# A fourth tile for outgoing attention rows, and a later place for the first expert's weights, in a kernel that runs banded attention and a top-1 mixture of experts

## The chip, the cores and the metric

The kernel runs on one core of one Trainium2 chip. The metric is the time of one execution in device microseconds. Three executions of the kernel before were timed, and one was taken by the hardware profiler.

## The reference

Attention first: 8 batches, 8 heads, 576 positions, head size 64. Heads 0 to 3 see the last 32 positions, heads 4 to 7 every fourth one of the last 128. The result, 4608 rows of 512, goes into a mixture of 8 experts: each row picks one.

```python
scores = scale * np.matmul(q, k.transpose(0, 1, 3, 2))
scores = np.where(masks[None], scores, -1e9)          # plain window, or dilated by 4
attn = np.exp(scores - scores.max(-1)); attn /= attn.sum(-1) + 1e-9
x = np.matmul(attn, v)  ->  [4608, 512]
logits = x @ w_gate + modality_bias[modality_id]      # [4608, 8]
e_idx = argmax(logits);  gate_w = softmax(logits)[e_idx]
for e in range(8):                                    # w1 [512, 1024], w2 [1024, 512] per expert
    out[mask] = gate_w[mask] * (np.maximum(x[mask] @ w1[e], 0) @ w2[e])
```

## The kernel before, in words

**Attention** is cut into 72 units, nine per batch (m = 0 to 8), and two units make a pair. A loop over `t` = 0 to 35 (and a few rounds more to drain) works three pairs at once: scores of pair t, exponentials of pair t - 1, products with V and normalization of pair t - 2. `state['t']` is 2t, so a time "62" in the code means pair 31. The order of PE, DVE, ACT and SP is written out by hand; each engine takes its instructions in that order.

In one round the order is: scores (PE) and the addition of the mask (DVE, L438); the product with V; loads of queries and of V for the next batch (SP); a first call of the background tasks (`advance`); the maximum (DVE, L444) with its subtraction on GpSimd; normalization (DVE, L399), which writes the rows into a tile `x_sb`; transposes of K and Q for the next batch (PE, L351, from the load tile `st`); copies (L514, L521, L149); a second and a third call of the background tasks around the turn of the probabilities; then `keep`, in which SP sends finished `x_sb` tiles to the buffers `x_dram` (L412 to L422); loads of K (SP); and a fourth call of the background tasks. So the rows of a pair are sent near the end of the round in which they are normalized. `x_sb` has three buffers and five are taken per batch; a new one can be written once the transfer out of the third one back has landed.

**Background tasks** do the gating of finished batches: they scatter each token into a list in DRAM (`table`). After batch 2, four early slots of 256 rows of one expert each are formed from what is known by then; the rest is routed after the last batch. A slot's rows come by indirect DMA into `xr`, go out to `x_slot` (L807), and come back as `xg` (L813) in another order; `prepare_x` transposes them on DVE (L962) and splits them into a high and a low part (L968, L971).

**The first slot** is served by `first_slot`, one of those background tasks: twelve steps of its weights are issued on SP at set times, by `load_more(0, 1)`, each of which runs the generator `fetch_weights` to its next `yield`. A step is either one quarter (256 KB) of a half of w1 (`half`, L828) or one pair of row blocks of w2 (`pair`, 512 KB, L833). The twelve steps are, in order: w2 pair 0; four quarters of w1's first half; w2 pairs 1 and 2; four quarters of w1's second half; w2 pair 3. While it waits for the next time, and once the time is past 63, the task also steps `prepare_x` for slot 0.

**Experts.** From pair 35 on, `slots` runs between attention's last instructions and then alone: per slot eight blocks f, each with twelve products for h and six for the output, in three terms of high and low parts. Weights are split on ACT (L980) and DVE (L981) just before use: block f uses a quarter of a half of w1 and half of a pair of w2. Weights of later slots are issued by `ahead` in the slot before, and are skipped where the expert stays the same.

**Queues.** All loads, weights and outgoing rows are issued on SP; only the gathers and scatters go through GpSimd.

Of the kernel before, what the change touches and what calls it, by code (L numbers as in the profile page):

```python
# [10 lines left out]
F32 = mybir.dt.float32  # L11
F32R = mybir.dt.float32r
BF16 = mybir.dt.bfloat16
I32 = mybir.dt.int32
# [8 lines left out]
B, H, S, D = 8, 8, 576, 64  # L23
NT = B * S
DM = H * D
NE = 8
# [9 lines left out]
GB = 96  # L36
NGB = S // GB
# [21 lines left out]
def kernel(  # L59
# [160 lines left out]


    nc.gpsimd.memset(gat.tile([P, 2, DM], F32, name="xr", bufs=1), 0.0)
    zero = cpool.tile([1, DM // 2], F32, name="zero")
    nc.gpsimd.memset(zero, 0.0)

    def constants():

        for _ in range(5):
            yield
        nc.scalar.copy(out=wgs[:, :, 0:NE], in_=wg)  # L230
        yield
        yield
        mid_t = spare[1][0:B, 0:S]
        for i in range(2):
            for a in range(2):
                nc.vector.tensor_copy(out=mid_t.rearrange("b (a c i j) -> b a i c j", a=2, c=2, i=2)[:, a, i],
                                      in_=mid[i][:, :, 0].rearrange("b (j c a) -> b a c j", c=2, a=2)[:, a])
        sent = spare[1][:, S:S + (NE + 1) * NT * 3 // P].bitcast(I32)
        nc.gpsimd.memset(sent, SENT)
        yield  # L240
        yield
        got = []

        def turn(po):
            for c in range(NGB):
                nc.tensor.transpose(out=po[0:GB, 1, ROUTE + B * c:ROUTE + B * (c + 1)], in_=mid_t[:, GB * c:GB * (c + 1)], identity=ident[:B, :B])
            got.append(po[0:GB, 1, ROUTE:ROUTE + NBLK])
        yield from on_po(turn)
        pm = got[0]
        mid_f = cpool.tile([GB, NBLK], F32, name="mid_f")  # L250
        nc.vector.tensor_copy(out=mid_f.rearrange("p (b c) -> p c b", c=NGB), in_=pm.rearrange("p (c b) -> p c b", b=B))
        yield
        yield
        mid_n = cpool.tile([GB, NBLK], F32, name="mid_n")
        nc.vector.tensor_scalar(out=mid_n, in0=mid_f, scalar1=-1.0, scalar2=1.0, op0=ALU.mult, op1=ALU.add)
        mtmp = spare[1][0:GB, S + (NE + 1) * NT * 3 // P:S + (NE + 1) * NT * 3 // P + NE * NBLK].rearrange("p (e c) -> p e c", c=NBLK)
        nc.gpsimd.tensor_tensor(out=mterm, in0=mid_n.rearrange("p (o c) -> p o c", o=1).broadcast_to([GB, NE, NBLK]),
                                in1=bias_sb[:, 0, :].rearrange("p (e o) -> p e o", o=1).broadcast_to([GB, NE, NBLK]), op=ALU.mult)
        nc.gpsimd.tensor_tensor(out=mtmp, in0=mid_f.rearrange("p (o c) -> p o c", o=1).broadcast_to([GB, NE, NBLK]),
                                in1=bias_sb[:, 1, :].rearrange("p (e o) -> p e o", o=1).broadcast_to([GB, NE, NBLK]), op=ALU.mult)  # L260
        nc.gpsimd.tensor_tensor(out=mterm, in0=mterm, in1=mtmp, op=ALU.add)
        yield
        yield
        nc.sync.dma_start(out=table.rearrange("(p a) t -> p (a t)", p=P), in_=sent)

        nc.gpsimd.iota(pay[:, :, 2], pattern=[[GB, NBLK]], base=0, channel_multiplier=1)
        place = cpool.tile([GB, 2, NBLK], I32, name="place")
        nc.gpsimd.iota(place[:, 0], pattern=[[0, B], [GB, NGB]], base=0, channel_multiplier=1)
        nc.gpsimd.iota(place[:, 1], pattern=[[S, B], [0, NGB]], base=0, channel_multiplier=0)
        ewt_i = cpool.tile([GB, NE, NGB], I32, name="ewt_i")  # L270
        nc.gpsimd.iota(ewt_i, pattern=[[-1, NE], [0, NGB]], base=NE, channel_multiplier=0)
        eoff_i = cpool.tile([GB, NE, NGB], I32, name="eoff_i")
        nc.gpsimd.iota(eoff_i, pattern=[[NT, NE], [0, NGB]], base=0, channel_multiplier=0)
        yield
        yield
        nc.vector.tensor_copy(out=ewt, in_=ewt_i)
        nc.vector.tensor_copy(out=eoff, in_=eoff_i)
        nc.gpsimd.memset(ones_bf, 1.0)
        nc.gpsimd.affine_select(out=upper, in_=ones_bf, pattern=[[1, GB]], compare_op=ALU.is_gt,
                                fill=0.0, base=0, channel_multiplier=-1)  # L280
        for t in x_dram:
            nc.sync.dma_start(out=t[NT:NT + 1, :], in_=zero)
        placef = cpool.tile([GB, 2, NBLK], F32, name="placef")
        nc.vector.tensor_copy(out=placef, in_=place)
        past = cpool.tile([GB, NBLK], F32, name="past")
        nc.vector.tensor_scalar(out=placef[:, 1], in0=placef[:, 0], scalar1=float(NCLS), scalar2=None, op0=ALU.mult)
        for r in range(1, NCLS):
            nc.vector.tensor_scalar(out=past, in0=placef[:, 0], scalar1=float(CL * r), scalar2=float(NCLS * CL - (2, -1, 2)[r - 1]), op0=ALU.is_ge, op1=ALU.mult)
            nc.vector.tensor_tensor(out=placef[:, 1], in0=placef[:, 1], in1=past, op=ALU.subtract)
        yield  # L290
        yield
        nc.vector.tensor_copy(out=place[:, 0], in_=placef[:, 1])
        nc.vector.tensor_tensor(out=pay[:, :, 0], in0=place[:, 0], in1=place[:, 1], op=ALU.add)
        yield
        yield
        nc.vector.tensor_copy(out=sid_all[:, :, 0], in_=sidx_i)
        nc.vector.tensor_scalar(out=sid_early[:, :, 0], in0=sid_all[:, 0:EARLY[0][1], 0], scalar1=-1.0, scalar2=float(EARLY[0][1] - 1), op0=ALU.mult, op1=ALU.add)
# [68 lines left out]
    class Unit:  # L366
# [23 lines left out]
        def finish(self, pov, den):  # L390
            if self.m in (1, 3, 6, 8):
                self.xs = state['xs']
            else:
                self.xs = state['xs'] = awk.tile([P, 2, 4 * D], F32, name="x_sb", bufs=3)
            if self.m < 5:
                xo = self.xs[:, self.m % 2].rearrange("p (a g d) -> p g a d", g=2, a=2)
            else:
                xo = self.xs.rearrange("p a (e g d) -> p e g a d", e=2, g=2)[:, self.hp]
            nc.vector.tensor_tensor(out=xo, in0=pov[:, :, 1:VB - 1].rearrange("p g (a d) -> p g a d", a=2),  # L399
                                    in1=den.rearrange("p g (a o) -> p g a o", o=1).broadcast_to([P, 2, 2, D]), op=ALU.mult)  # L400
# [416 lines left out]
    def fetch_weights(si, first):  # L817

        e = nc.sync.value_load(si[0:1, 0:1], min_val=0, max_val=NE - 1)
        kw = {}  # L820
        if not first:
            kw = dict(cond=nc.sync.value_load(si[0:1, 2:3], min_val=0, max_val=1), cond_hint=False)
        w1v = w1[ds(e, 1)].rearrange("o (r m p) f -> (o r) p m f", r=KC, p=BLK)

        def half(i):
            cols = slice(HALFF * P * i, HALFF * P * (i + 1))
            for r in range(KC):
                nc.sync.dma_start(out=w1q[i][BLK * r:BLK * (r + 1)], in_=w1v[r, :, :, cols], **kw)  # L828
                if first and r < KC - 1:
                    yield  # L830

        def pair(c):
            nc.sync.dma_start(out=w2q[c], in_=w2[ds(e, 1), 2 * P * c:2 * P * (c + 1), :].rearrange("o (a p) m -> p (o a) m", p=P), **kw)  # L833
            yield from ()

        for piece, i in ((pair, 0), (half, 0), (pair, 1), (pair, 2), (half, 1), (pair, 3)):
            yield from piece(i)
            yield

# [30 lines left out]
    def load_more(n, pieces):  # L870

        if n not in loads_of and n in si_of:
            loads_of[n] = [fetch_weights(si_of[n], n == 0), 0]
        if n in loads_of:
            for _ in range(min(pieces, 6 - loads_of[n][1])):
                next(loads_of[n][0], None)
                loads_of[n][1] += 1

    def first_rows(n, at):
# [7 lines left out]
        fetching.extend([(n, rows)] * n)  # L887
        todo['rows'] = max(todo['rows'], n + 1)

    def first_slot():  # L890

        prep = prepare_x(0, ids_of[0])
        for n, at in enumerate((46, 50, 52, 54, 56, 60, 62, 64, 65, 66, 67, 68)):
            while state['t'] < at:
                if state['t'] > 63:
                    next(prep, None)
                yield
            load_more(0, 1)
            loads_of[0][1] = max(n - 5, 1)
            yield  # L900
        yield from prep

# [257 lines left out]
    for t in range(NPAIR + 4):  # L1160
# [81 lines left out]
        if 0 <= t - 2 < NPAIR:  # L1242
            for unit in pairs[t - 2].units:
                unit.keep(nc.sync)
        load_next(t, here, k)
        advance([*round_of, B - 1] if moe and here else range(-1, B))
        if t == NPAIR + 2:
            octx.close()
# [45 lines left out]
```

## Time and profile before

| | |
|---|---|
| three executions | 693.64, 702.48, 708.86 us (median 702.48) |
| profiled execution, its own time | 694.29 us |
| its span, first to last instruction | 692.3 us |
| granted TensorE clock, mean | 0.969 |
| PE / PEld / DVE / ACT / POOL busy | 94 / 82 / 70 / 56 / 37 % |
| DMA | 131,677 packets, 99.12 MB, mean 143 GB/s |

PE is TensorE's matmuls and PEld its weight loads, DVE is VectorE, ACT ScalarE, POOL GpSimd, SP SyncE. A row of a timeline has the start, the time, engine, line, operation, output and input, and in brackets how long the engine stood idle before it and what ended that. A row of waits has the sum, how often, and the longest. Lines are those of the kernel before.

### The profile page before, as it was taken

How to read it: one execution, taken by the hardware profiler on the slowest of the kernel's cores; microseconds unless marked ns; L12 is line 12 of the kernel's file. 1: busy time of each engine (PE TensorE's matmuls, PEld its weight loads, DVE VectorE, ACT ScalarE, POOL GpSimd, SP SyncE). 2: the span in 40 equal slices, each digit the busy share in tenths (PEclk: the TensorE clock that was granted, in tenths of full speed). 3: DMA queues.
4: the chain of work that ended last, by engine and by line, in shares of the span. 5: the costliest groups of instructions: out<-in, count | busy, mean ns of one | idle time of the engine just before them, and what ended most of it. 6: DMA issues, size and time to landing. Idle time of an engine off the chain costs nothing. (4 is left out here: it accounts for less than half of the span.)

```text
span 692.3 us, 17695 instructions
## 1 busy us (share of the span) xinstructions
PE 648.2 (94%) x6462; PEld 566.8 (82%) x6462; DVE 483.4 (70%) x1074; ACT 384.5 (56%) x754; POOL 259.5 (37%) x315
## 2 busy tenths in 40 slices
PE   7899999998968899869999999999999999999994
PEld 4688887887757788759999999899999999889983
DVE  4768878887746866936766686667766776677652
ACT  1646765665534545434666565565666566556552
POOL 8423555645645635743312331333223341311110
PEclk9989999999978999998999999999999999999998
DMA  9966879879897434775322336743232326921560
GB/s 201 219 182 174 218 131 214 205 137 208 191 221 210 136 52 101 152 164 171 113 72 77 107 121 170 213 108 123 73 102 86 107 95 151 254 95 63 134 163 12
DMA packets 131677, 99.12 MB, mean 143 GB/s; under 512 B 67760, under 2 KB 111794, under 8 KB 131588
## 3 DMA queue, kind: packets, MB, share of 16 engines
q1 hardware_dynamic: 120500, 78.11, 46.5%
q0 software_dynamic: 8048, 19.20, 9.6%
q8 instruction: 52, 0.85, 0.5%
q10 hardware_dynamic: 3040, 0.65, 0.5%
q14 instruction: 37, 0.30, 0.2%
HBM read 127.52 MB, written 29.39 MB: 227 GB/s over the span
## 5 line engine op out<-in xcount | busy, mean ns | idle before, releaser
L981 DVE TENSOR_TENSOR w2l<-w2q,w2h 128x512 fp32r<-128x512 f32 x152 | 104.8, 689 | 41.7 <-ACT w2h L980 34.0
L1012 PE MATMUL py<-w2h,hh 128*128 128x512 f32 x296 | 119.3, 403 | 0.0
L1012 PE MATMUL py<-w2h,hl 128*128 128x512 f32 x296 | 117.5, 397 | 0.0
L313 POOL DMA_INDIRECT xr<-x_dram,idt x74 | 81.4, 1100 | 94.3 <-DMA x_slot<-xr 44.3
L313 POOL DMA_INDIRECT out_dram<-ys,idt x37 | 42.4, 1145 | 198.2 <-ACT ys L1015 122.1
L1012 PE MATMUL py<-w2l,hh 128*128 128x512 f32 x296 | 116.2, 392 | 0.0
L981 DVE TENSOR_TENSOR w1l<-w1q,w1h 128x512 fp32r<-128x512 f32 x152 | 103.8, 684 | 12.5 <-ACT w1h L980 12.5
L980 ACT CAST w1h<-w1q 128x512 fp32r<-128x512 f32 x152 | 94.6, 622 | 13.4 <-DMA w1q<-in_moe_w_dram 13.4
L1032 PE MATMUL pt<-xh,w1h 128*128 128x256 f32 (+1 forms) x320 | 91.4, 286 | 6.7 <-ACT w1h L980 6.7
L980 ACT CAST w2h<-w2q 128x512 fp32r<-128x512 f32 x152 | 93.1, 613 | 0.0
L1032 PE MATMUL pt<-xh,w1l 128*128 128x256 f32 (+1 forms) x320 | 91.4, 286 | 1.0 <-DVE w1l L981 1.0
L1032 PE MATMUL pt<-xl,w1h 128*128 128x256 f32 (+1 forms) x320 | 90.7, 283 | 0.0
L1032 PE MATMUL ph<-xh,w1l 128*128 128x256 f32 (+1 forms) x288 | 81.1, 282 | 1.7 <-DVE w1l L981 1.6
L1032 PE MATMUL ph<-xl,w1h 128*128 128x256 f32 (+1 forms) x288 | 80.9, 281 | 0.0
L1032 PE MATMUL ph<-xh,w1h 128*128 128x256 f32 (+1 forms) x288 | 80.8, 281 | 0.0
L1038 ACT ACTIVATE hh<-pt 128x256 fp32r<-128x256 f32 (+1 forms) x80 | 30.3, 378 | 88.5 <-PE pt L1032 88.5
L313 POOL TENSOR_TENSOR sm<-sm,nmx 128x768 f32<-128x768 f32 x36 | 52.9, 1470 | 57.2 <-DVE den L469 38.5
L1032 PEld LDWEIGHTS pt<-xh,w1h 128*128 128x128 f32 x320 | 61.3, 192 | 11.0 <-ACT w1h L980 7.3
L1038 ACT ACTIVATE hh<-ph 128x256 fp32r<-128x256 f32 (+1 forms) x72 | 27.1, 377 | 76.8 <-PE ph L1032 76.8
L1012 PEld LDWEIGHTS py<-w2l,hh 128*128 128x128 f32 x296 | 56.1, 190 | 13.9
L1032 PEld LDWEIGHTS pt<-xl,w1h 128*128 128x128 f32 x320 | 61.3, 192 | 3.1
L1032 PEld LDWEIGHTS pt<-xh,w1l 128*128 128x128 f32 x320 | 61.5, 192 | 2.0 <-DVE w1l L981 2.0
(197 smaller groups left out, 1304.7 us busy)
## 6 DMA issues: line engine op xcount, KB each, us to landing
w2q<-in_moe_w_dram SPq DMA_DIRECT2D x76, 512.0 KB
w1q<-in_moe_w_dram SPq DMA_DIRECT2D x152, 256.0 KB
x_slot<-xr SPq DMA_DIRECT2D x18, 512.0 KB
xg<-x_slot SPq DMA_DIRECT2D x72, 128.0 KB
x_dram<-x_sb SPq DMA_DIRECT2D x32, 256.0 KB
st<-in_k_dram SPq DMA_DIRECT2D x32, 144.0 KB
vw<-in_v_dram SPq DMA_DIRECT2D x16, 288.0 KB
st<-in_k_dram SPq DMA_DIRECT2D x8, 576.0 KB
```

Source lines behind the costliest of these rows:

```text
L313: ins = tc.keep_in_program_order(getattr(nc.gpsimd, name)(*args, **kw))
L980: nc.scalar.copy(out=hi, in_=raw)
L981: nc.vector.tensor_tensor(out=lo, in0=raw, in1=hi.bitcast(F32), op=ALU.subtract)
L1012: nc.tensor.matmul(out=py[u], lhsT=ht[:, us], rhs=wt, start=(f + n == 0), stop=(f + n == FC + 1))
L1032: nc.tensor.matmul(out=ph, lhsT=wt[:, c, :], rhs=xt[:, c, 0:cols], start=(c + i == 0), stop=(c + i == KC + 1))
L1038: nc.scalar.activation(out=hh, in_=ph, func=AF.Relu)
```

## The change

`x_sb` gets four buffers instead of three. The room for it comes from small tiles of the setup (`mid_f`, `mid_n`, `place`, `ewt_i`, `eoff_i`, `placef`, `past`), which now lie in w1's first buffer behind the modality ids, and from the row of zeros, which is now read from the tile of the warm-up products.

The first slot's steps come in a new order, at new times, and from another place. Order: four quarters of w1's first half, w2 pair 0, four quarters of w1's second half, w2 pairs 1, 2 and 3. They are issued by `first_weights`, which runs near the end of a round, after `keep` and the load of K and before the fourth call of the background tasks. The task `first_slot` only fills the list of times and, once the time is past 63, steps `prepare_x` at each call.

| step | before, round t | after, round t |
|---|---|---|
| w1 first half, 4 quarters | 25, 26, 27, 28 | 24, 25, 26, 27 (ends) |
| w2 pair 0 | 24 | 31 (end) |
| w2 pairs 1, 2 | 30, 31 | 34 (end) |
| w1 second half, 4 quarters | 32, 33, 33, 34 | 32, 32, 33, 33 (ends) |
| w2 pair 3 | 34 | 34 (end) |

```diff
-    zero = cpool.tile([1, DM // 2], F32, name="zero")
-    nc.gpsimd.memset(zero, 0.0)
+    zero = warm[0:1].bitcast(F32)
+    room = [S * 2]
+
+    def setup(shape, dtype):
+
+        n = shape[1] * (shape[2] if len(shape) > 2 else 1)
+        room[0] += n
+        t = spare[0][0:shape[0], room[0] - n:room[0]]
+        t = t if dtype is F32 else t.bitcast(dtype)
+        return t.rearrange("p (a b) -> p a b", a=shape[1]) if len(shape) > 2 else t
...
-        mid_f = cpool.tile([GB, NBLK], F32, name="mid_f")
+        mid_f = setup([GB, NBLK], F32)
...
-                self.xs = state['xs'] = awk.tile([P, 2, 4 * D], F32, name="x_sb", bufs=3)
+                self.xs = state['xs'] = awk.tile([P, 2, 4 * D], F32, name="x_sb", bufs=4)
...
-        for piece, i in ((pair, 0), (half, 0), (pair, 1), (pair, 2), (half, 1), (pair, 3)):
+        order = ((half, 0), (pair, 0), (half, 1), (pair, 1), (pair, 2), (pair, 3)) if first else ((pair, 0), (half, 0), (pair, 1), (pair, 2), (half, 1), (pair, 3))
+        for piece, i in order:
             yield from piece(i)
             yield
...
+    ending = []
+
+    def first_weights():
+
+        while ending and ending[0][1] <= state['t']:
+            load_more(0, 1)
+            loads_of[0][1] = max(ending.pop(0)[0] - 5, 1)
+
     def first_slot():
 
         prep = prepare_x(0, ids_of[0])
-        for n, at in enumerate((46, 50, 52, 54, 56, 60, 62, 64, 65, 66, 67, 68)):
-            while state['t'] < at:
-                if state['t'] > 63:
-                    next(prep, None)
-                yield
-            load_more(0, 1)
-            loads_of[0][1] = max(n - 5, 1)
+        ending.extend(enumerate((46, 50, 52, 54, 62, 64, 64, 66, 66, 68, 68, 68)))
+        while len(ending) > 3:
+            if state['t'] > 63:
+                next(prep, None)
             yield
         yield from prep
...
         load_next(t, here, k)
+        first_weights()
         advance([*round_of, B - 1] if moe and here else range(-1, B))
```

More of the change, by code (lines that the diff above doesn't have):

```diff
@@ L253, in constants @@
         yield
-        mid_n = cpool.tile([GB, NBLK], F32, name="mid_n")
+        mid_n = setup([GB, NBLK], F32)
         nc.vector.tensor_scalar(out=mid_n, in0=mid_f, scalar1=-1.0, scalar2=1.0, op0=ALU.mult, op1=ALU.add)
@@ L266, in constants @@
         nc.gpsimd.iota(pay[:, :, 2], pattern=[[GB, NBLK]], base=0, channel_multiplier=1)
-        place = cpool.tile([GB, 2, NBLK], I32, name="place")
+        place = setup([GB, 2, NBLK], I32)
         nc.gpsimd.iota(place[:, 0], pattern=[[0, B], [GB, NGB]], base=0, channel_multiplier=1)
         nc.gpsimd.iota(place[:, 1], pattern=[[S, B], [0, NGB]], base=0, channel_multiplier=0)
-        ewt_i = cpool.tile([GB, NE, NGB], I32, name="ewt_i")
+        ewt_i = setup([GB, NE, NGB], I32)
         nc.gpsimd.iota(ewt_i, pattern=[[-1, NE], [0, NGB]], base=NE, channel_multiplier=0)
-        eoff_i = cpool.tile([GB, NE, NGB], I32, name="eoff_i")
+        eoff_i = setup([GB, NE, NGB], I32)
         nc.gpsimd.iota(eoff_i, pattern=[[NT, NE], [0, NGB]], base=0, channel_multiplier=0)
@@ L282, in constants @@
             nc.sync.dma_start(out=t[NT:NT + 1, :], in_=zero)
-        placef = cpool.tile([GB, 2, NBLK], F32, name="placef")
+        placef = setup([GB, 2, NBLK], F32)
         nc.vector.tensor_copy(out=placef, in_=place)
-        past = cpool.tile([GB, NBLK], F32, name="past")
+        past = setup([GB, NBLK], F32)
         nc.vector.tensor_scalar(out=placef[:, 1], in0=placef[:, 0], scalar1=float(NCLS), scalar2=None, op0=ALU.mult)
```

## The prediction

> **What bounds the kernel now.** I read the page first (which engine is full), then the stages, then the waits, then the timeline around the longest wait.
>
> ```profile
> span 692.3 us, 17695 instructions
> PE 648.2 (94%) x6462; PEld 566.8 (82%) x6462; DVE 483.4 (70%) x1074; ACT 384.5 (56%) x754; POOL 259.5 (37%) x315
> ```
> ```profile
> 65.00:151.00 86.00, 83.42 (x1587) 71.75 (x1577) 73.20 (x212) 55.54 (x102) 45.46 (x59) 1.00 0.82 179
> 151.00:219.00 68.00, 55.87 (x960) 47.29 (x958) 42.66 (x115) 33.02 (x59) 35.54 (x44) 0.90 0.90 209
> 340.00:692.00 352.00, 341.83 (x2189) 308.73 (x2188) 240.22 (x423) 205.86 (x426) 89.44 (x81) 0.99 0.41 117
> ```
>
> The columns are the stretch, its length, PE, PEld, DVE, ACT and POOL busy, then PE's granted clock, the DMA share and GB/s. PE sets the time in most of the run: from 340 us on it is busy 341.83 of 352. No line of the change works there. The one long stretch with room is the second half of attention, 151 to 219: PE is idle 68.00 - 55.87 = **12.1 us**, the clock falls to 0.90, and the DMA engines are busy 0.90 of the time. Between 65 and 151, with the same work and no weights, PE was idle 2.6 of 86. So 12.1 us, plus what the clock costs, is all that this change can win.
>
> The pairs of units show the same. One score addition (L438) opens each pair t = 0 to 35:
>
> ```profile
> 65.40 0.96 DVE L438 TENSOR_TENSOR sm<-pss,masks 128x768 f32<-128x768 f32 x1
> ...
> 150.92 0.96 DVE L438 TENSOR_TENSOR sm<-pss,masks 128x768 f32<-128x768 f32 x1
> ...
> 194.05 0.96 DVE L438 TENSOR_TENSOR sm<-pss,masks 128x768 f32<-128x768 f32 x1
> ...
> 209.20 0.96 DVE L438 TENSOR_TENSOR sm<-pss,masks 128x768 f32<-128x768 f32 x1 [2.71 <-PE pss L436]
> ...
> 218.78 0.95 DVE L438 TENSOR_TENSOR sm<-pss,masks 128x768 f32<-128x768 f32 x1
> ...
> 229.15 0.95 DVE L438 TENSOR_TENSOR sm<-pss,masks 128x768 f32<-128x768 f32 x1
> ```
>
> These are pairs 9, 24, 31, 32, 33 and 35. From 9 to 24 a pair takes 85.5 / 15 = 5.7 us; from 24 to 31, 43.1 / 7 = 6.2; pair 31 takes 15.2 and pair 32 takes 9.6. The waits of DVE and PE in attention say on what:
>
> ```profile
> DVE x_sb L399 <- DMA x_dram<-x_sb: 13.8, 7, 6.1
> ```
> ```profile
> PE pss L351 <- DMA st<-in_k_dram: 3.9, 1, 3.9
> PE pss L351 <- DMA st<-in_q_dram: 1.6, 2, 1.4
> ```
> ```profile
> 155.25 0.42 DVE L399 TENSOR_TENSOR x_sb<-po,den 128x256 f32<-128x256 f32 x1 [1.51 <-DMA x_dram<-x_sb]
> ...
> 173.61 0.76 DVE L399 TENSOR_TENSOR x_sb<-po,den 128x256 f32<-128x256 f32 x2 [2.80 <-DMA x_dram<-x_sb]
> ...
> 204.28 0.42 DVE L399 TENSOR_TENSOR x_sb<-po,den 128x256 f32<-128x256 f32 x1 [6.10 <-DMA x_dram<-x_sb]
> ...
> 210.26 0.95 DVE L444 TENSOR_REDUCE nmx<-sm 128x8 f32<-128x768 f32 x1
> ...
> 212.92 0.76 DVE L149 COPY vw<-vw 32x520 f32<-32x520 f32 x2
> 216.77 0.71 DVE L962 STREAM_TRANSPOSE xt<-xg 128x512 f32<-128x512 f32 x1 [3.09 <-DMA xg<-x_slot]
> ```
> ```profile
> 201.19 0.87 PE L351 MATMUL pss<-ident,st 96*128 96x96 f32 x4 [3.90 <-DMA st<-in_k_dram]
> 203.47 0.90 PE L351 MATMUL pss<-ident,st 96*128 96x96 f32 x4 [1.42 <-DMA st<-in_q_dram]
> ```
>
> DVE stops 13.8 us in seven places because the third tile back has not been written out. But at the longest, 6.10 until 204.28, PE stands too, for keys until 201.19 and queries until 203.47. **Two waits lie side by side there, and both are for the same queue.** What fills it is in SP's order of issue (start, SP's time in the issue):
>
> ```profile
> 161.02 0.39 SPq L833 DMA_DIRECT2D w2q<-in_moe_w_dram  x1
> ...
> 192.44 0.42 SPq L121 DMA_DIRECT2D st<-in_k_dram  x1
> 192.95 0.56 SPq L121 DMA_DIRECT2D st<-in_q_dram  x1
> ...
> 195.33 0.40 SPq L833 DMA_DIRECT2D w2q<-in_moe_w_dram  x1
> ...
> 206.22 0.38 SPq L807 DMA_DIRECT2D x_slot<-xr  x1
> 206.81 0.40 SPq L833 DMA_DIRECT2D w2q<-in_moe_w_dram  x1
> ...
> 209.60 2.46 SPq L813 DMA_DIRECT2D xg<-x_slot  x4
> ...
> 222.62 0.39 SPq L833 DMA_DIRECT2D w2q<-in_moe_w_dram  x1
> ```
>
> The last keys are issued at 192.44 and used at 201.19: about 8.7 us in a queue that is full.
>
> **The change part by part.** It adds no instruction and no DMA; it takes one memset of 256 numbers off POOL. Everything else is order and room.
>
> The fourth tile. Each output tile may now wait for the fourth tile back, whose transfer was issued one or two pairs before. I expect all seven waits of L399 to go. What that is worth has two ends. Low: at 204.28 only what lies behind PE's last wait goes, 204.28 - 203.47 = **0.8 us**, and the other 13.8 - 6.1 = 7.7 us that are won earlier are lost again at 203.47, since the loads do not come sooner. High: 7.7 + 0.8 = 8.5, if SP, which also follows the pairs, issues those loads as much sooner. The nearest row is the DMA share of 0.90 in 151 to 219: a lead turns into an earlier landing only where the queue has gaps. I take 0.8 + 1.8 = 2.6, near the low end.
>
> pair 0 of w2, 0.52 MB at 161.02, goes behind the last load (after pair 31). The four pieces of w1's first half stay in the same pairs, some half a pair earlier, after the outgoing rows instead of before them, so they neither add nor remove bytes ahead of the last keys. At the 209 GB/s of 151 to 219, 524,288 bytes are **2.5 us** that the last keys and queries land earlier. The low end is 0 (it went out 31 us before those loads; gaps in between may swallow it), the high end 2.8 at the 186 GB/s of this row:
>
> ```profile
> 169.00:176.00 7.00, 4.69 (x75) 3.82 (x71) 3.98 (x11) 3.42 (x9) 5.73 (x7) 0.96 1.09 186
> ...
> 194.00:209.00 15.00, 9.68 (x110) 7.94 (x110) 4.79 (x14) 4.73 (x8) 4.78 (x6) 0.68 0.98 262
> ```
>
> The Trainium skill's page "DMA: Bandwidth & Descriptors", section Specifications, gives a core about 358 GB/s from memory. By that, 0.52 MB would be an estimated 1.5 us and the sum below 4.1; the trace doesn't agree, since a stage with a DMA share of 0.98 moved 262.
>
> pair 1 (195.33) was issued behind the last keys, so it delays only what follows: the last V load, x_slot and through it xg. Without it xg lands up to 2.5 us earlier relative to the keys. Against that stands a step that is easy to overlook: the new loop asks for the first slot's transposition at the **first** call of pair 32 instead of the second (the old loop spent that call on a weight piece). L962 then stands in DVE's order before the maximum, normalization and copies of that pair, not after them. What is queued behind its wait is nmx, x_sb, lT and vw: from 210.26, just after the score addition of pair 32, to 212.92 + 0.76 = 213.68, so 3.4 us, of which POOL's subtraction, ACT's exponentials and PE's turn of the rows wait. Before, 2.0 us passed from the transposition (216.77) to the next score addition (218.78); after, 0.7 + 3.4 = 4.1, so **+2.1**. Against -2.5 I put the two together at 0; ends -2.5 and +2.1.
>
> Pairs 1, 2 and 3 and the second half of w1 now go out after pairs 32 to 34, 1.5 MB at once at the end. Their use:
>
> ```profile
> L980 ACT CAST w1h<-w1q x24: 610/621/624, 227.9 to 318.1; 128x512 fp32r<-128x512 f32 x24
> ```
> ```profile
> L980 ACT CAST w2h<-w2q x22: 602/612/624, 233.7 to 317.6; 128x512 fp32r<-128x512 f32 x22
> ```
>
> The split of w1 begins at 227.9 with the half that is long there. 1.57 MB at the slowest rate above, 186, take 8.5 us, from about 223 to 232; w2 is first split at 233.7, and that is pair 0, which is ahead of them. So cost 0; if attention ended ten microseconds sooner, this cover would be gone and ACT would wait for pair 1. The setup tiles lie in w1's first buffer, long free by the time its weights come, and the zero row is read from the warm-up tile: 0.
>
> **Sum:** 0.8 + 1.8 + 2.5 + 0 = 5.1 us off the attention part. Everything after it starts from its end, so I carry it through: 694.3 (the profiled execution's own time) - 5.1 = 689.2. That execution is at the fast end of the runs, 693.64, 702.48 and 708.86: their median is 1.2% above it, and 702.5 - 5.1 = 697.4. The next three may fall the same way; from the mean of the three, 701.7, comes 696.6, and I say **696**.
>
> **The rivals.** *The wait changes its name.* The x_sb waits go, PE waits as long for keys and queries, and the gaps swallow pair 0: 0.8 us, 693.5 (701.7 from the median). For it: the two waits side by side, and the share of 0.98. The same size comes out if the gain is given back at the next place that waits on a fixed chain:
>
> ```profile
> 297.07 0.36 SPq L784 DMA_DIRECT2D idt<-table  x1
> ...
> 310.31 0.58 PE L1032 MATMUL pt<-xh,w1h 128*128 128x256 f32 x1 [6.65 <-ACT w1h L980]
> ```
>
> There PE stands 6.65 us because SP had first to read the routed list. Against it: the list is made from attention's last batch, so it moves along.
>
> *All the idle time goes.* If loads follow the pairs, the 12.1 us go whole: 682.2 (690.4). For it: PE waited for keys only once in all of attention, so without the stalls the queue may never have filled. Against it: 0.90 share over 68 us.
>
> *The clock stays up.* From 194 to 209 PE's clock was 0.68, 15 x 0.32 = 4.8 us of lost clock. If the shorter stalls leave the clock alone, this comes on top: 5.1 + 4.8 = 9.9, so 684.4 (692.6). The Trainium skill's page "TensorE: Matmul & The Clock Gate", Part 1, has the clock fall to half after an idle window of some 3.4 us and come back after as long a busy one; the idle of 3.90 and the low clock beside it agree. Against: I leave part of the stall standing.
>
> *DVE blocks on xg* (slower). If xg lands when it does now, because it hangs on SP's queue and not on the pairs, all that was won before is lost at L962, and the 2.1 us of the new place are paid: 696.4 against 694.3 (704.6 against the median). It decides from the point where xg lands less than 2.1 us earlier than 216.77. For it: DVE waited 3.09 already at the later place, and x_slot, 512 KB of pair 0 and xg still follow each other. Against: pair 1 is out of the way.
>
> **How the numbers follow.** Forecast (3 to 7 us won) 0.45; the wait changes its name 0.22; all idle 0.08; the clock 0.08; DVE on xg 0.12; 0.05 for what I don't see. No case reaches 2% of the time, 14 us, which is about what a measurement of this kernel can tell from no change; only the two large ones come near, and the spread of the runs before (15 us) carries some over: faster by over 2% 0.10, within 0.86, slower by over 2% 0.04. The range goes from 685, where the large cases end between the two bases, to 705, the slower rival from the median.
>
> **What would show it.** No wait of L399 for x_dram<-x_sb; the wait of L351 for keys still there but ending sooner; L438 of pair 32 about 5 us earlier, near 204; L962 waiting right behind that L438 for 3 to 5 us; no wait of ACT for w1q or w2q before 260; POOL, PE and DVE after 340 as they are. I am wrong if L351 waits to 203 as now (first rival), if pair 33 isn't earlier (DVE on xg), or if the stall around 303 to 310 grows by what attention gained.

## The result, and the profile after

The kernel after the change took 707.62 us in the median of four executions (703.84, 708.0, 707.23, 709.91), against 700.75 for the kernel before on the same chip. The ratio is 1.0148, 95% interval 1.0102 to 1.0194: 1.5% slower, within 2% of no change but on the other side of it from the forecast; the 707.62 lie 11.6 us above the 696 and above the range's 705. On another chip the same two kernels stood at 692.96 and 691.41, ratio 1.0047 (1.0008 to 1.0086). The ratios are taken over the fast executions alone and so are not the quotients of the medians (here 1.0098). By both intervals the change is slower, on the second chip only just; by how much is not settled. The profiled execution took 703.84 us. Lines after line 220 stand 8 to 14 further down: L446 is the score addition that was L438, L407 is L399, L359 is L351, L976 is L962.

The head of the page of the kernel after, and three stretches, with the columns of the prediction:

```profile
span 701.8 us, 17694 instructions
PE 658.5 (94%) x6461; PEld 572.6 (82%) x6462; DVE 482.2 (69%) x1074; ACT 384.9 (55%) x754; POOL 258.3 (37%) x314
```
```profile
65.00:151.00 86.00, 81.19 (x1409) 68.39 (x1409) 63.72 (x190) 50.03 (x91) 43.85 (x56) 0.94 0.82 177
151.00:219.00 68.00, 58.67 (x995) 49.41 (x995) 42.98 (x120) 34.66 (x63) 33.72 (x42) 0.94 0.78 177
340.00:701.00 361.00, 351.79 (x2258) 318.43 (x2256) 248.12 (x436) 213.23 (x440) 92.36 (x83) 0.99 0.41 117
```

The work is the same but for one memset (17,694 instructions). From 151 to 219 PE is busier than before (58.67 against 55.87 of 68) and the DMA engines have room (0.78 against 0.90). That the change relieved the queue does not follow: in its second profile (below) the DMA share between the openings of pairs 24 and 32 is 0.93, against 0.90 and 0.91 in the two profiles of before. And from 65 to 151, where only the tiles differ (the fourth `x_sb` and the setup's), PE got through 1,409 matmuls where it had 1,587, but through 1,625 in the change's second profile. So fixed stretches can't be compared, and the profile has to be divided by pairs. The score additions of pairs 24, 32, 33 and 35 on DVE's timeline, with what stands between the last three:

```profile
156.80 0.96 DVE L446 TENSOR_TENSOR sm<-pss,masks 128x768 f32<-128x768 f32 x1 [0.50 <-ACT ux L490]
...
209.55 0.96 DVE L446 TENSOR_TENSOR sm<-pss,masks 128x768 f32<-128x768 f32 x1 [0.40 <-ACT ux L490]
218.10 0.71 DVE L976 STREAM_TRANSPOSE xt<-xg 128x512 f32<-128x512 f32 x1 [7.59 <-DMA xg<-x_slot]
...
219.99 0.76 DVE L407 TENSOR_TENSOR x_sb<-po,den 128x256 f32<-128x256 f32 x2
...
224.44 0.96 DVE L446 TENSOR_TENSOR sm<-pss,masks 128x768 f32<-128x768 f32 x1 [0.60 <-PE pss L444]
...
236.53 0.91 DVE L446 TENSOR_TENSOR sm<-pss,masks 128x768 f32<-128x768 f32 x1
```

Before, these four pairs opened at 150.92, 209.20, 218.78 and 229.15. The 703.84 - 694.29 = 9.55 us between the two profiled executions divide so: up to pair 24, 156.80 - 150.92 = 5.9 us; from 24 to 32, 52.75 against 58.28, **5.5 us won**; from 32 to 35, 26.98 against 19.95, **7.0 us lost**; after pair 35, 703.84 - 236.53 = 467.3 against 465.1, 2.2 us. Divided so, the change wins about what was forecast for it and gives it back in the next three pairs. The 5.9 us ahead of pair 24 are another matter (see the open points).

What DVE waits for at L976 stands in SP's order of issue of the kernel after:

```profile
205.77 0.38 SPq L815 DMA_DIRECT2D x_slot<-xr  x1
...
208.87 0.41 SPq L841 DMA_DIRECT2D w2q<-in_moe_w_dram  x1
209.38 3.75 SPq L821 DMA_DIRECT2D xg<-x_slot  x4
```

x_slot and xg are a chain of two transfers. xg is issued at 209.38, as before (209.60), and 512 KB of weights now stand directly ahead of it; before, they went out at 206.81, while x_slot was on its way. DVE asks at about 210.5, just after the score addition of pair 32, instead of 213.7. PE's timeline and its clock show who pays:

```profile
220.47 0.90 PE L487 MATMUL pt<-ident,x_sb 128*128 128x128 f32 x3 [6.88 <-DVE x_sb L407]
```
```profile
217.00:218.00 1.00, 0.00 (x0) 0.00 (x0) 0.00 (x0) 0.00 (x0) 0.00 (x0) 1.00 0.04 8
218.00:219.00 1.00, 0.00 (x0) 0.00 (x0) 0.90 (x2) 0.15 (x1) 0.00 (x0) 0.59 0.00 0
...
221.00:222.00 1.00, 1.00 (x19) 0.70 (x19) 0.93 (x4) 0.54 (x2) 0.84 (x2) 0.50 0.66 223
...
230.00:231.00 1.00, 1.00 (x24) 0.87 (x26) 0.81 (x2) 1.00 (x3) 0.11 (x1) 0.50 1.01 253
231.00:232.00 1.00, 1.00 (x30) 0.78 (x24) 0.24 (x1) 0.68 (x1) 0.57 (x2) 0.58 1.02 221
232.00:233.00 1.00, 1.00 (x34) 0.93 (x32) 0.90 (x2) 0.00 (x0) 0.68 (x1) 1.00 0.49 123
```

PE waits 6.88 us for the rows that DVE holds back. Its clock falls to 0.50 at about 218.2 and stays there until about 231.8, eleven microseconds after PE is at work again.

### The profile page after: what moved, and what is told of

The parts are those of the page before. It is cut to its first block, busy times and chain, and to the rows that moved or that the text cites. A ratio compares the mean times of both kernels' runs of the same rounds, so it can differ in the third digit from the quotient of the medians.

```text
span 701.8 us, 17694 instructions
## 1 busy us (share of the span) xinstructions
PE 658.5 (94%) x6461; PEld 572.6 (82%) x6462; DVE 482.2 (69%) x1074; ACT 384.9 (55%) x754; POOL 258.3 (37%) x314
## 5 line engine op out<-in xcount | busy, mean ns | idle before, releaser
L321 POOL DMA_INDIRECT xr<-x_dram,idt x74 | 83.3, 1126 | 96.0 <-DMA x_slot<-xr 58.2
L321 POOL DMA_INDIRECT out_dram<-ys,idt x37 | 40.2, 1086 | 192.2 <-ACT ys L1029 119.7
L1053 DVE SCALAR_TENSOR_TENSOR hl<-ph,hh 128x256 fp32r<-128x256 f32 (+1 forms) x72 | 30.0, 417 | 48.7 <-ACT hh L1052 45.6
```

Of the source, the lines that this page charges most:

```text
L321: ins = tc.keep_in_program_order(getattr(nc.gpsimd, name)(*args, **kw))
L1053: nc.vector.scalar_tensor_tensor(out=hl, in0=ph, scalar=0.0, in1=hh.bitcast(F32), op0=ALU.max, op1=ALU.subtract)
```

## The experiments

Three theories of the loss were set against each other. Theory A: DVE waits for xg at its new, earlier place, and the engines that need DVE's results wait behind it. Theory B: the weights that now go out in one bunch at the end make the experts start late. Theory C: the fourth tile, or the setup's tiles in w1's buffer, cost something. A time ratio is always against the kernel before on the same chip; the first four runs shared one chip, the next four a second, the last four a third.

**The tile alone** (`x_sb` and the setup's tiles as after; the old weights and `first_slot`):

```diff
-  self.xs = state['xs'] = awk.tile([P, 2, 4 * D], F32, name="x_sb", bufs=3)
+  self.xs = state['xs'] = awk.tile([P, 2, 4 * D], F32, name="x_sb", bufs=4)
```

> The fourth tile and the moved setup tiles alone; the first slot's weights as before. Before took 698.4 us as a mean of its undisturbed runs, the change 1.48% more. Theory A (the loss is DVE standing at L962 for xg at the first call of pair 32, 7.59 us in the profile after against 3.09 before): the tile is harmless, 695 to 700 us, ratio 0.995 to 1.003. Theory B (the weights that go out in a bunch after pairs 32 to 34 hold up what follows): also 695 to 700. Theory C (the fourth tile itself costs, because attention's stalls move from DVE to places that are worse): 703 or more, ratio over 1.007. In all of them no wait of L399 for x_dram is left.

Measured 0.9991 (0.9960 to 1.0023), nothing either way. C falls. No wait for x_dram is left, and still pairs 24 to 32 took 58.4 us, as before: the waits went, the time didn't.

**The weights alone** (the change with `bufs=3`):

```diff
-  name="x_sb", bufs=4)
+  name="x_sb", bufs=3)
```

> The change with three tiles instead of four: new order, times and place of the first slot's weights alone. Theory A and theory B: 705 to 711 us, ratio 1.010 to 1.018, with the wait of DVE for xg at 6 us or more in pair 32. Theory C: back to 695 to 700. In all, the waits of L399 for x_dram return, but less than 13.8 us, since 0.5 MB less is ahead of them.

Measured 1.0101 (1.0054 to 1.0148): the loss is in this half. DVE's wait for x_dram fell to 1.1 us without a fourth tile. That moving the weights did this is not shown: in a profile with the old weights and three tiles (the transposition at the first call, below) it is 2.3 us. DVE waits 7.9 us for xg.

**The change, with the transposition asked for at the second call of pair 32**, as before:

```diff
+        calls = 0
         while len(ending) > 3:
             if state['t'] > 63:
-                next(prep, None)
+                calls += 1
+                if calls > 1:
+                    next(prep, None)
```

> The change, but with the transposition for the first slot asked for at the second call of pair 32, as before the change, not the first. Theory A: most of the loss goes, 697 to 701 us, ratio 0.998 to 1.004, and pair 32 takes under 11 us instead of 14.9. Theory B: 705 to 709, since the bunch of weights is as it was. Theory C: 703 to 707.

Measured 1.0068 (1.0028 to 1.0109). The wait for xg fell to 4.69 us and pairs 32 to 35 to 22.9, but the kernel is still slower than before. This is a miss for A, by which most of the loss should have gone: the second call alone does not bring it back.

**The kernel before, with the transposition at the first call of pair 32**:

```diff
             load_more(0, 1)
             loads_of[0][1] = max(n - 5, 1)
+            if state['t'] > 63:
+                next(prep, None)
             yield
```

> The kernel before, with the transposition for the first slot asked for at the first call of pair 32 and nothing else changed. Theory A: the loss appears without the change, 702 to 707 us, ratio 1.005 to 1.013, and DVE waits 6 us or more for xg right behind the score addition of pair 32. Theories B and C: as before, ratio 0.997 to 1.003.

Measured 1.0026 (0.9989 to 1.0064): a second miss for A, which expected 1.005 to 1.013; no loss is shown, and none over 0.6% is likely. The execution that was profiled, 707.36 us, was the longest of twelve (median 699.08), so of its timeline only the stage in question is read:

```profile
164.62 0.96 DVE L438 TENSOR_TENSOR sm<-pss,masks 128x768 f32<-128x768 f32 x1 [0.50 <-ACT ux L482]
...
217.30 0.96 DVE L438 TENSOR_TENSOR sm<-pss,masks 128x768 f32<-128x768 f32 x1 [0.39 <-ACT ux L482]
226.13 0.71 DVE L964 STREAM_TRANSPOSE xt<-xg 128x512 f32<-128x512 f32 x1 [7.87 <-DMA xg<-x_slot]
...
244.56 0.91 DVE L438 TENSOR_TENSOR sm<-pss,masks 128x768 f32<-128x768 f32 x1
```

With the old weights and three tiles, the earlier question alone brings a wait of 7.87 and 244.56 - 217.30 = 27.3 us for pairs 32 to 35, as much as the whole change in its own profiles (27.0 and 28.5). But pairs 24 to 32 took 52.7 us here, against 58.3 in the first profile of before, although up to pair 32 the two programs are the same. So from 24 to 35 nothing is lost (79.9 against 78.2, and 81.2 in the second profile of before): how such a stretch divides at pair 32 differs from execution to execution.

**The change, with the transposition asked for only from pair 33 on**:

```diff
-            if state['t'] > 63:
+            if state['t'] > 65:
```

> The change, with the first slot's transposition asked for from pair 33 on, one round later than at the second call. At the second call the change still was at ratio 1.0068, with DVE standing 4.69 us for xg and pair 32 at 12.6 us. Theory A (what is lost is DVE in front of xg, which lands late because pair 0 of w2 now goes out just ahead of it): no wait for xg is left, pairs 32 and 33 take under 13 us together instead of 22.2 in the profile after, and the whole is at 692 to 699 us, ratio 0.992 to 1.001. Theory B (the late bunch of weights costs by itself, behind attention's end): 702 to 706, ratio 1.005 to 1.010, with the loss after pair 35.

Measured **0.9911** (0.9871 to 0.9952), 685.78 us against 691.32. One number turns the slower kernel into one that beats both.

```profile
155.03 0.96 DVE L446 TENSOR_TENSOR sm<-pss,masks 128x768 f32<-128x768 f32 x1 [0.50 <-ACT ux L490]
...
204.81 0.96 DVE L446 TENSOR_TENSOR sm<-pss,masks 128x768 f32<-128x768 f32 x1 [0.40 <-ACT ux L490]
...
213.84 0.71 DVE L976 STREAM_TRANSPOSE xt<-xg 128x512 f32<-128x512 f32 x1 [1.27 <-DMA xg<-x_slot]
...
224.64 0.91 DVE L446 TENSOR_TENSOR sm<-pss,masks 128x768 f32<-128x768 f32 x1
```

Pairs 24 to 32 took 49.8 us, 32 to 35 took 19.8. And the bunch of weights at the end is all there: 687.51 - 224.64 = 462.9 us for the rest, no more than the 465.1 of before. B falls as the cause.

**The same, with pair 0 of w2 behind xg** (at time 64 instead of 62; one quarter of w1 moves from 64 to 66 with it):

```diff
-  (46, 50, 52, 54, 62, 64, 64, 66, 66, 68, 68, 68)
+  (46, 50, 52, 54, 64, 64, 66, 66, 66, 68, 68, 68)
```

> As the run with the transposition from pair 33, and pair 0 of w2 also issued after xg (end of pair 32, not 31). Theory A: xg lands some 2 us sooner, but nothing waits for it any more, so the same as that run within 2 us. Theory B: also the same, 702 to 706; if pair 0 is late for its split, ACT waits for w2q near pair 35 and it is slower by that.

Measured 0.9941 (0.9907 to 0.9974), not told apart from the run before it; the wait for xg is 3.01 us and not shorter. A miss: with pair 0 out of its way, xg was not awaited less.

**Four tiles, the old weights, the transposition from pair 33 on** (the edit is against the tile alone):

```diff
-                if state['t'] > 63:
+                if state['t'] > 65:
                     next(prep, None)
                 yield
             load_more(0, 1)
             loads_of[0][1] = max(n - 5, 1)
+            if state['t'] > 65:
+                next(prep, None)
             yield
```

> Four tiles, the first slot's weights in the old order and at the old times, transposition from pair 33 on. It shows whether moving the weights is worth anything once xg is out of the way. With four tiles, the old weights and the old second call the ratio was 0.9991 and pair 32 took 8.4 us. Theory A: 694 to 699, ratio 0.994 to 1.000, level with the run that moves the weights or up to 5 us above it (pair 32 opened at 209.5 and 211.4 with the weights moved, at 215.2 without). Theory B: 694 to 699 and clearly below the run that moves the weights.

Measured 0.9968 (0.9935 to 1.0). Against 0.9911 with the moved weights the intervals overlap: that moving the weights is worth something on top is likely, not shown.

**The kernel before, unchanged**, for a second profile of it:

> The kernel before again, for a second profile of it. All four experiments have nearly the same course of pairs 8 to 30 (pair 12 at 7.3 us, pair 22 at 8.6 to 10.9), and the first profile of before has another (5.0 and 6.2). Either theory: 692 to 705 us. If the course of the first profile comes again, the changes made the difference; if that of the experiments comes, the first profile was one of several courses that the same program can take, and pairs 8 to 31 of single profiles can't be compared.

695.33 us. On DVE's timeline pairs 24, 32 and 35 and the waits:

```profile
152.17 0.96 DVE L438 TENSOR_TENSOR sm<-pss,masks 128x768 f32<-128x768 f32 x1
...
211.44 0.96 DVE L438 TENSOR_TENSOR sm<-pss,masks 128x768 f32<-128x768 f32 x1 [2.69 <-PE pss L436]
...
220.00 0.71 DVE L962 STREAM_TRANSPOSE xt<-xg 128x512 f32<-128x512 f32 x1 [4.09 <-DMA xg<-x_slot]
...
233.37 0.95 DVE L438 TENSOR_TENSOR sm<-pss,masks 128x768 f32<-128x768 f32 x1
```
```profile
DVE x_sb L399 <- DMA x_dram<-x_sb: 15.1, 6, 5.0
```

The picture of the prediction again: 15.1 us of waits for x_dram, 59.3 us from 24 to 32, and 21.9 from there to 35.

**The change, unchanged**:

> The changed kernel again, beside the versions below on one chip, and a second profile of it. Theory A (DVE stands in front of xg in pair 32, and PE behind DVE): ratio 1.010 to 1.019 as on record; pairs 32 and 33 take 20 us or more together and the wait for xg is 6 us or more, as in the first profile (22.2 and 7.59). If they take 15 or less while the ratio stays, theory A is wrong for the size of the loss.

Measured 1.0047 (1.0008 to 1.0086), below the 1.010 to 1.019 that was expected; the waits are as A has them. DVE's timeline, PE's wait, and SP's issues:

```profile
145.73 0.96 DVE L446 TENSOR_TENSOR sm<-pss,masks 128x768 f32<-128x768 f32 x1
...
198.24 0.96 DVE L446 TENSOR_TENSOR sm<-pss,masks 128x768 f32<-128x768 f32 x1 [1.52 <-ACT ux L490]
208.81 0.71 DVE L976 STREAM_TRANSPOSE xt<-xg 128x512 f32<-128x512 f32 x1 [9.61 <-DMA xg<-x_slot]
...
226.70 0.91 DVE L446 TENSOR_TENSOR sm<-pss,masks 128x768 f32<-128x768 f32 x1
```
```profile
211.18 0.90 PE L487 MATMUL pt<-ident,x_sb 128*128 128x128 f32 x3 [9.35 <-DVE x_sb L407]
```
```profile
197.77 0.38 SPq L815 DMA_DIRECT2D x_slot<-xr  x1
...
200.97 0.40 SPq L841 DMA_DIRECT2D w2q<-in_moe_w_dram  x1
203.78 1.78 SPq L821 DMA_DIRECT2D xg<-x_slot  x4
```

Pairs 24 to 32 took 52.5 us, and then DVE stands 9.61 us and PE 9.35. From the issue of x_slot to the use of xg are 208.81 - 197.77 = 11.0 us, and DVE stands there from 198.24 + 0.96 = 199.20 on, 1.4 us after the start of that chain.

**The change, with pair 0 directly behind x_slot**, in the gap in which before had a pair:

```diff
         while len(ending) > 3:
+            if state['t'] == 62 and ending[0][0] == 4:
+                first_weights()
```

> The change, with pair 0 of w2 issued right behind x_slot, in the time in which SP waits for x_slot to land, where pair 2 stood before the change, and not at the end of pair 31 just ahead of xg. The transposition stays at the first call. Theory A with the queue's share: xg lands about 2 us sooner after the opening of pair 32 (8.5 us in the profile after, 7.5 before), the wait falls from 7.6 to about 5.5, ratio 1.007 to 1.013. If pair 0's place doesn't matter, 7 to 8 us of wait and 1.010 to 1.019.

Measured 1.0024 (0.9982 to 1.0066): not told apart from the change or from before. The wait for xg is 4.19 us instead of 9.61, and pairs 32 to 35 take 22.7, but pairs 24 to 32 now take 57.2. Only 1.4 us of the shorter wait come from the chain, which takes 207.37 - 197.73 = 9.6 us from the issue of x_slot to the use of xg instead of 11.0. The other 4.0 come from pair 32, which opens 4.5 us behind the issue of x_slot instead of 0.5.

```profile
197.73 0.38 SPq L815 DMA_DIRECT2D x_slot<-xr  x1
```
```profile
207.37 0.71 DVE L978 STREAM_TRANSPOSE xt<-xg 128x512 f32<-128x512 f32 x1 [4.19 <-DMA xg<-x_slot]
```

**The change, with the transposition only from the third call of pair 33 on**:

```diff
-        while len(ending) > 3:
-            if state['t'] > 63:
+        calls = 0
+        while state['t'] < 68:
+            calls += state['t'] > 65
+            if calls > 2:
                 next(prep, None)
             yield
+        next(prep, None)
         yield from prep
```

> The change, with the first transposition at the third call of pair 33, half a round after the run from pair 33 on (ratio 0.9911), in which DVE still stood 1.27 us for xg, and 3 to 4.6 us in its two neighbours. Theory A: no wait for xg, pair 33 at 5 to 6 us instead of 7.7; 0.986 to 0.992. If the splits of the rows come too late for the first slot, ACT or PE wait for xh near pair 35 and it is slower than 0.9911.

Measured 0.9925 (0.9887 to 0.9963). No wait for xg; no better than from the first call of pair 33.

**The transposition from pair 33 on, and x_slot and xg issued earlier** (at times 60 and 62):

```diff
-  first_rows(0, (t0 + 12, t0 + 13, t0 + 16, t0 + 17, t0 + 18, t0 + 20, t0 + 22))
+  first_rows(0, (t0 + 12, t0 + 13, t0 + 16, t0 + 17, t0 + 18, t0 + 18, t0 + 20))
```

> The change with the transposition from pair 33 on, and x_slot and xg issued one round earlier (x_slot at the third call of pair 30, xg at the first call of pair 31). Theory A: no wait for xg at all, 0.986 to 0.992. Against: SP reaches x_slot before its rows have been gathered or xg before x_slot has landed, and stands with the last loads of V behind it; then PE waits for V in pair 34 and it is above 0.9911.

Measured 0.9915 (0.9877 to 0.9953), on the chip on which the change stands at 1.0047. The data are there when they are asked for, as the transposition behind the score addition of pair 33 shows: it stands in the timeline with no wait.

```profile
146.95 0.96 DVE L446 TENSOR_TENSOR sm<-pss,masks 128x768 f32<-128x768 f32 x1 [0.86 <-ACT ux L490]
...
202.74 0.96 DVE L446 TENSOR_TENSOR sm<-pss,masks 128x768 f32<-128x768 f32 x1 [0.40 <-ACT ux L490]
...
208.40 0.96 DVE L446 TENSOR_TENSOR sm<-pss,masks 128x768 f32<-128x768 f32 x1 [0.37 <-ACT ux L490]
209.28 0.70 DVE L976 STREAM_TRANSPOSE xt<-xg 128x512 f32<-128x512 f32 x1
...
220.06 0.91 DVE L446 TENSOR_TENSOR sm<-pss,masks 128x768 f32<-128x768 f32 x1
```

All profiles side by side, each length from two score additions, the rest as the execution's time less the opening of pair 35:

| kernel | DVE first asks for xg | waits for it | 24 to 32 | 32 to 35 | 24 to 35 | rest | ratio |
|---|---|---|---|---|---|---|---|
| before | pair 32, 2nd call | 3.1 | 58.3 | 20.0 | 78.2 | 465.1 | 1 |
| before again | pair 32, 2nd | 4.1 | 59.3 | 21.9 | 81.2 | 462.0 | 1 |
| tile alone | pair 32, 2nd | none | 58.4 | 18.7 | 77.1 | 464.0 | 0.9991 |
| change, 2nd call | pair 32, 2nd | 4.7 | 55.2 | 22.9 | 78.1 | 467.0 | 1.0068 |
| before, 1st call | pair 32, 1st | 7.9 | 52.7 | 27.3 | 79.9 | 462.8 | 1.0026 |
| weights alone | pair 32, 1st | 7.9 | 55.6 | 27.3 | 82.9 | 464.5 | 1.0101 |
| change | pair 32, 1st | 7.6 | 52.8 | 27.0 | 79.7 | 467.3 | 1.0148 |
| change again | pair 32, 1st | 9.6 | 52.5 | 28.5 | 81.0 | 465.0 | 1.0047 |
| change, pair 0 in the gap | pair 32, 1st | 4.2 | 57.2 | 22.7 | 79.9 | 465.1 | 1.0024 |
| change, pair 33 | pair 33, 1st | 1.3 | 49.8 | 19.8 | 69.6 | 462.9 | 0.9911 |
| the same, pair 0 behind xg | pair 33, 1st | 3.0 | 52.7 | 22.1 | 74.9 | 466.3 | 0.9941 |
| old weights, pair 33 | pair 33, 1st | 4.6 | 51.7 | 22.1 | 73.8 | 463.9 | 0.9968 |
| change, third call | pair 33, 3rd | none | 51.5 | 19.2 | 70.7 | 468.0 | 0.9925 |
| xg early, pair 33 | pair 33, 1st | none | 55.8 | 17.3 | 73.1 | 465.6 | 0.9915 |

The column 24 to 35 divides the kernels without overlap: 77.1 to 82.9 where DVE asks in pair 32, 69.6 to 74.9 where it asks later, and every ratio below 0.997 belongs to the second group. So what stands of A is this: in the changed kernel the question in pair 32 costs, and one round later it does not. In three forms (a question in pair 33, one two calls later, and one in pair 33 with earlier data) the gain is there, 5 to 6 us of some 691. That the step from the second to the first call is the whole loss, as A had it, is not shown: both runs that move only this step missed, and over 24 to 35 the two calls lie at 77.1 to 81.2 and 79.7 to 82.9.

## Why the prediction was wrong, point by point

**The waits for x_dram**: right that all seven would go. They are absent from the change, and even the tile alone has none. The tile alone brought nothing measurable, so the low end, 0.8, was nearer than the 2.6 that were taken. The waits are also no fixed property of the old kernel: with its tiles and weights, and the transposition at the first call, one profile has 2.3 us of them instead of 13.8.

**Pair 0 behind the last loads, 2.5 us**: no run isolates it. Without the two kernels that move other transfers too (pair 0 in the gap, xg early), the kernels with both halves need 49.8 to 55.2 us for pairs 24 to 32, mean 52.4; the three profiles of before's weights with three tiles 52.7 to 59.3, mean 56.7. The lead of 4.3 us is near the 5.1 of the sum, but it is not shown: the ranges overlap, and two kernels that are the same program up to pair 32 (the tile alone; old weights, pair 33) took 58.4 and 51.7.

**The failing step is the term of xg**: "Against -2.5 I put the two together at 0; ends -2.5 and +2.1". Pairs 32 to 35 take 27.0 to 28.5 us, mean 27.5, in the four kernels that ask at the first call with xg's place in the queue unaided, and 18.7 to 22.9, mean 20.9, in the four that ask at the second. **Measured from pair 32 on the term is +6.6, not 0**, three times the worst end. A part of that comes from measuring at pair 32, since the kernels that ask later also reached pair 32 later: over pairs 24 to 35 the two groups have means of 80.9 and 78.7. That whole stretch shows what the step did to the sum: the change takes 79.7 and 81.0 us, before 78.2 and 81.2, where 5.1 less was forecast, and with the question one round later the change takes 69.6. Three things were wrong in the term.

- The -2.5. Pair 1 went away ahead of xg, but the chain from the issue of x_slot to the use of xg did not get shorter: 12.3 and 11.0 us in the change's profiles, 10.6 and 12.7 in those of before. Pair 0 now stands directly ahead of xg, where the old pair stood in the gap behind x_slot; the change's own table, read against SP's order, would have shown that. Whether this place is the reason is open: in the gap again the chain took 9.6 us, with pair 0 behind xg 13.5.
- The point of comparison. The prediction carried xg along with attention. But x_slot is issued at the end of pair 31's work, in the second profile of the change only 0.5 us ahead of pair 32's score addition (3.8 in the first), and xg is two transfers behind it. The chain has a length of its own, 11.0 us there, and DVE, which asks 1.4 us after its start, waits for the rest.
- The price. "What is queued behind its wait" named DVE's 3.4 us and left out PE, which stands 6.88 to 9.35 us for `x_sb`, and the clock that falls meanwhile. From the transposition (218.10) to the next score addition (224.44) passed 6.3 us where 4.1 were worked out, and pair 33 behind it ran at 0.50 to its end (pair 34 opens at 231.76). The prediction used the clock only as a gain, in the rival "The clock stays up"; here it was a price too, since PE was made to stand. By the Trainium skill's page "TensorE: Matmul & The Clock Gate", Part 1, an idle window of about 3.4 us halves the clock. In the first profile the trace agrees: PE stood 6.88 us and the clock fell to 0.50, 4.6 us after PE stopped at 213.6. In the second it fell sooner than the page has it, at about 204.1 (mean 0.53 from 204 to 205), some 2.2 us after PE stopped at 201.8.

**The bunch of weights, 0**: about right. The rest of the run is 465.7 in the mean of the nine kernels with the late bunch and 463.6 in the five with the old weights; some 2 us of cost aren't excluded, and the shortest of the nine, 462.9, is below the 465.1 of the first profile of before.

**The sum**: with +6.6 in the place of 0 it is 6.6 - 5.1 = 1.5 us slower, ratio 1.002. That lies in the interval of the second chip (1.0008 to 1.0086), not in that of the first (1.0102 to 1.0194). The rival "DVE blocks on xg" named the place, its waiting row, and 696.4, 0.3% above the profiled time; it got 0.12 and deserved most of the chance, for what spoke for it was in the trace (a wait of 3.09 at the later place), and what spoke against it was only that pair 1 had gone.

**The signs**: no x_dram wait, right; PE's wait for keys still there but ending sooner, not quite: it is gone, and queries are awaited instead in the second profile (3.83 us at most); pair 32 near 204, missed in the first profile (209.55), and 198.24 in the second; the wait right behind it 3 to 5 us, wrong (7.59 and 9.61); pair 33 isn't earlier (224.44 against 218.78), which was the sign given for the rival. No wait of ACT for weights before 260, right. The stall of PE near 303 to 310 did not grow: 2.41 and 6.34 us, against 6.65.

**What stays open.** On the first chip the loss is 1.5%, on the other 0.5%. Of the first profile's 9.55 us, 5.9 lie ahead of pair 24, where only the tiles differ. The same program opened pair 24 at 145.73 in its second profile, 11 us sooner; and the kernel before with the transposition at the first call, in which no tile of the setup has moved, opened it at 164.62. So neither the change nor its tiles are needed for a late opening; whether chips differ, or executions of one program do, wasn't tried. Nor is it explained why the change with the second call stays at 1.0068 with 78.1 us from 24 to 35. And no run issues x_slot and xg earlier while DVE asks in pair 32, so whether the wait or the place of the transposition's work in pair 32 costs more is not separated; what the traces show is the wait, and PE's behind it.

## What to carry to other kernels

Where a step of another task is inserted into an engine's fixed order, ask what its data wait for and when that chain *begins*; work around it that gets faster can bring the question ahead of the data. An instruction that waits on a DMA in such an order holds up the engines behind it too, and here the matmul clock after it. A gain that vanishes in the next stage is best found by dividing both profiles at the same landmarks and subtracting, stage by stage; here that pointed at one number in the code, and with it the ratio went from 1.0047 (1.0008 to 1.0086) to 0.9911 (0.9871 to 0.9952), on two chips. One profile of each kernel is not enough for it: parts that are the same program differed by up to 6.7 us from pair 24 to 32.

## What the hardware showed that was not expected

In these traces the matmul clock did not come back soon after PE had work again. In the change's first profile PE works from 220.47 on, and the clock is at 0.50 until about 231.8, 11 us; in the second it works from 211.18, and these rows show the clock still at half nine microseconds later:

```profile
220.00:221.00 1.00, 1.00 (x9) 0.67 (x11) 0.99 (x3) 0.85 (x1) 0.00 (x0) 0.50 0.87 274
221.00:222.00 1.00, 1.00 (x38) 0.88 (x40) 0.59 (x3) 1.00 (x3) 0.27 (x1) 0.93 0.95 256
```

The Trainium skill's page "TensorE: Matmul & The Clock Gate", Part 1, has full clock again after some 3.4 us of sustained work, and the prediction repeated it. In these two stretches the measurement differs, by a factor of three. In the first profile of before it is about 6 us: PE works from 203.47, and the clock is full from about 209.5. What PE does in these stretches (small products with short gaps, and turns of rows) may be why, which no run here separates.

And PE was slow in one place without a wait that the profile shows. In the first profile of the change, products with V come in groups of four to six with gaps that no semaphore explains, while the DMA engines are full:

```profile
194.20 0.37 PE L472 MATMUL po<-vw,pT 96*64 96x65 f32 x5 [0.40 <-issue]
194.94 0.37 PE L472 MATMUL po<-vw,pT 96*64 96x65 f32 x5 [0.37 <-issue]
```
```profile
194.00:197.00 3.00, 1.67 (x24) 1.26 (x26) 0.44 (x1) 0.20 (x1) 1.35 (x2) 1.00 1.07 246
```

PE is busy 1.67 of 3 us at full clock, DMA share 1.07. That the one causes the other is not shown.
